# Final parameter products in wide views, log dt gradient as rows, w2 loads without touches: a joint forward and backward kernel on one core

## The chip, the cores and the metric

The kernel runs on one core of a Trainium2 chip. The metric is the device time of one execution in microseconds. TensorE multiplies matrices, VectorE and ScalarE work element by element, GpSimd (POOL in the profile) does some small element work and issues DMAs from a queue of its own, SyncE (SP) only issues DMAs, and ScalarE (ACT) can issue them as well.

## The reference

One call computes a forward pass and all gradients. The sizes are L = 2048 positions, D = 576 channels, N = 128 states and F = 4608 hidden units, and all tensors are bf16.

```python
xn = layernorm(x)                                     # over D
K[d, l] = Re sum_n C[d,n] * exp(dt[d]*A[d,n]*l) * dt[d]*B[d,n]   # dt = exp(log_dt), complex
s = causal_convolution(xn, K) + xn * Dskip            # along L, by FFT
h = silu(xn @ w1) * (xn @ w3)
out_0 = x + s * silu(h @ w2)
out_1 .. out_12 = gradients of out_0 against grad_out by
    x, A_re, A_im, B_re, B_im, C_re, C_im, log_dt, Dskip, w1, w3, w2
```

The gradients of A, B, C and log_dt end in small products. Four sums over the positions, S1 and S2 with real and imaginary parts, are made for each channel and state; out_2 to out_7 (576 x 128 each) are complex products of them with A, B, C and dt, and out_8 (576 values) is a sum over the states.

## The kernel before

All work is written once, stage by stage, for a list scheduler. `self.at(us)` gives the instructions that follow a planned time, and the scheduler puts each engine's instructions into an order by these times and by the dependences; on the chip each engine runs its list in that order. DMAs wait in the list of the engine that issues them (SP, POOL or ACT), and each of these has one queue.

The positions are 16 tiles of 128, D is five blocks of 128 channels (the last has 64), and F is 36 chunks of 128. The stages and the times they have in the profiled execution are these.

- *Prologue, 0 to 150 us.* Layer norm, the rates and the matrices of the Fourier transform.
- *Hidden layer and convolution kernel, 150 to 542.* `ffn_hidden` makes the two hidden products (matmul L719, gate tile `gu_t`, whose stores to `GI_dram` are issued by POOL, L728; hidden tile `h_t`, stored by SP). Beside it `ssm_kernel(0, 8.55)` generates the convolution kernel in 36 chunks that are planned 8.55 us apart; its last matmul (L500) ends at 516 us, and the hidden layer's last at 542.
- *Forward tail, 545 to 812.* `forward_tail` loads w2 in nine groups of four chunks (`w2g`, 590 KB each, issued by POOL, L771), loads the hidden tiles transposed (`hc`, SP), multiplies (`po`, L787), and makes the convolution in quarters (`spectra_quarter`, L609 and L582, with loads `cu`, L660, issued by POOL). A store of out_0 for each pair of tiles is issued by POOL, L849. The tile `goT` is cleared by POOL (L764) after the hidden layer, and the one-element copy L770 reads it.
- *Backward groups, 812 to 1647.* Gradients of w2, w1 and w3 (L1229, L1257, L1276), the backward convolution, and from 1331 us on the first 19 of 36 parameter chunks.
- *Input gradient, 1647 to 2017.* `phase6_inputs` makes 144 matmuls for each of the 16 tiles (L1336) into `px` or `pgw`, from transposed loads `guc` and `ggc` on SP. After a tile is done, VectorE adds it (L1346) and `ln_bwd_tile` makes the layer norm backward (L1376 to L1384) and stores out_1 from ACT (L1386). Between the matmuls stand the remaining 17 parameter chunks: 32 small matmuls each (L989) into `et_ps`, products on VectorE (L996, `pr_q`) and sums (L998) into `S_all`.
- *Final blocks.* `final_block` is a generator, one for each of the five blocks of channels, run at the chunk after which its sums are complete: block 0 after chunk 20, 3 after 30, 1 after 33, 2 and 4 after chunk 35, the last. It loads six `rates` (POOL, L1019), transposes the four sums (TensorE, L1023), copies them (ACT, L1025), makes the complex products one 128x128 plane at a time (VectorE, L1033 to L1038, scalings L1049, L1051, L1054), scales the outputs (VectorE, L1043 and L1045, into `gout`, two buffers) and stores them (POOL, L1016). The log dt gradient is collected as a column for each block in `glogdt`. After block 4 it is cast (L1074) and stored by two DMAs (POOL, L1077 and L1078) whose destination has consecutive 2-byte values on consecutive partitions.

The wait of the late w2 loads is written as a touch of the destination, which reads a tile that is cleared only after the hidden layer:

```python
if n >= 3:
    nc.vector.tensor_copy(out=t_[rem:rem + 1, 0, 0:1], in_=self.goT[0][rem:rem + 1, nfull, 0:1])
```

Of the kernel before, what the change touches and what calls it, by code (L numbers as in the profile page):

```python
# [60 lines left out]
class K:  # L61
# [669 lines left out]
    def forward_tail(self, T0, TB, TQ, gctx):  # L731
# [35 lines left out]
        for n, t_ in enumerate(w2g):  # L767
            self.at(T0 - 4 + 2.5 * n)
            if n >= 3:
                nc.vector.tensor_copy(out=t_[rem:rem + 1, 0, 0:1], in_=self.goT[0][rem:rem + 1, nfull, 0:1])  # L770
            nc.gpsimd.dma_start(out=t_[:], in_=aps["B_w2"][n * GRP * P:(n + 1) * GRP * P, :].rearrange(  # L771
                "(c p) d -> p c d", p=P))
# [53 lines left out]
        for i in range(LT):  # L826
# [15 lines left out]
            if i % 2 == 1:  # L842
# [3 lines left out]
                g_t = g_all[:, i0:i0 + 2, :]  # L846
                nc.vector.tensor_tensor(out=g_t, in0=g_t, in1=x_t[:], op=ALU.add)
                self.at(T0 + 54 + TB * i)
                nc.gpsimd.dma_start(out=out0[i0 * P:(i0 + 2) * P, :].rearrange("(t p) d -> p t d", p=P), in_=g_t)  # L849
# [17 lines left out]
    def ssm_bwd_params(self, chunk_at, final_at, out, big, S_all, ps):  # L867
        cfg = self.cfg
        D, LT = cfg.D, cfg.LT
        final = self.phase5_final(out, big, S_all, ps)  # L870
        with self.tc.tile_pool(name="g_k", bufs=1, side="right") as gkp, self.tc.tile_pool(name="g_t", bufs=3, side="right") as tqp, \
# [7 lines left out]
            for ch in range(D // 16):  # L879
                self.at(chunk_at(ch))  # L880
                self.param_chunk(ch, gz, S_all, tqp, qp, rp, ps)
                for c in final_at.get(ch, ()):
                    self.at(final_at[ch][c])
                    next(final[c])

# [115 lines left out]
    def phase5_final(self, out, big, S_all, ps2):  # L1001
        cfg = self.cfg
        fp = out.enter_context(self.tc.tile_pool(name="gf", bufs=1, side="right"))
        fo = out.enter_context(self.tc.tile_pool(name="gfo", bufs=2, side="right"))
        self.glogdt = big.tile([P, cfg.DT], FP32, name="glogdt")
        self.nc.vector.memset(self.glogdt[:], 0.0)
        self.rdt = big.tile([P, 1], FP32, name="rdt")
        return [self.final_block(c, do, dsz, fp, fo, big, S_all, ps2) for c, (do, dsz) in enumerate(cfg.dch)]

    def final_block(self, c, do, dsz, fp, fo, big, S_all, ps2):  # L1010
# [4 lines left out]
        tt, ts_ = nc.vector.tensor_tensor, nc.vector.tensor_scalar  # L1015
        store = lambda name, t_: nc.gpsimd.dma_start(out=aps[name][do:do + dsz, :], in_=t_[v])  # L1016
# [3 lines left out]
        Ar, Ai, Br, Bi, Cr, Ci = [rates[v, j] for j in range(6)]  # L1020
# [5 lines left out]
        S1r, S2r, S1i, S2i = [ST[v, k, :] for k in range(4)]  # L1026
        f = [fp.tile([P, N], FP32, name=f"f{n}")[v] for n in range(5)]
        acc = [fp.tile([P, 1], FP32, name=f"acc{n}")[v] for n in range(4)]
        dtc = self.dt_col[v, c:c + 1]
        Wr, Wi, t1, x, y = f  # L1030

        def pair(o, a, b, p, q, op):
            tt(out=o, in0=a, in1=b, op=ALU.mult)  # L1033
            tt(out=t1, in0=p, in1=q, op=ALU.mult)  # L1034
            tt(out=o, in0=o, in1=t1, op=op)  # L1035

        def dot(o, a, b):
            nc.vector.tensor_tensor_reduce(out=t1, in0=a, in1=b, scale=1.0, scalar=0.0, op0=ALU.mult, op1=ALU.add, accum_out=o)  # L1038

        def out_(o, name, neg):  # L1040
            ob = fo.tile([P, N], BF16, name="gout")
            if neg:
                ts_(out=ob[v], in0=o, scalar1=dtc, scalar2=-1.0, op0=ALU.mult, op1=ALU.mult)  # L1043
            else:
                ts_(out=ob[v], in0=o, scalar1=dtc, scalar2=None, op0=ALU.mult)  # L1045
            store(name, ob)

        pair(Wr, Cr, Br, Ci, Bi, ALU.subtract)
        ts_(out=Wr, in0=Wr, scalar1=dtc, scalar2=None, op0=ALU.mult)  # L1049
        pair(Wi, Cr, Bi, Ci, Br, ALU.add)  # L1050
        ts_(out=Wi, in0=Wi, scalar1=dtc, scalar2=None, op0=ALU.mult)  # L1051
        pair(x, Wr, S2r, Wi, S2i, ALU.subtract)
        pair(y, Wr, S2i, Wi, S2r, ALU.add)
        ts_(out=y, in0=y, scalar1=-1.0, scalar2=None, op0=ALU.mult)  # L1054
        out_(x, "out_2", False)
        out_(y, "out_3", False)
        dot(acc[0], x, Ar)
        dot(acc[1], y, Ai)
        tt(out=acc[0], in0=acc[0], in1=acc[1], op=ALU.add)
        dot(acc[2], S1r, Wr)  # L1060
        dot(acc[3], S1i, Wi)
        tt(out=acc[2], in0=acc[2], in1=acc[3], op=ALU.subtract)
        nc.vector.reciprocal(out=self.rdt[v], in_=dtc)
        tt(out=acc[2], in0=acc[2], in1=self.rdt[v], op=ALU.mult)
        tt(out=acc[0], in0=acc[0], in1=acc[2], op=ALU.add)
        tt(out=self.glogdt[v, c:c + 1], in0=acc[0], in1=dtc, op=ALU.mult)
        for (Xr, Xi, on_r, on_i) in ((Br, Bi, "out_6", "out_7"), (Cr, Ci, "out_4", "out_5")):
            pair(x, S1r, Xr, S1i, Xi, ALU.subtract)
            pair(y, S1r, Xi, S1i, Xr, ALU.add)
            out_(x, on_r, False)  # L1070
            out_(y, on_i, True)
# [409 lines left out]
```

## Time and profile before

| | us |
|---|---|
| time, median of three runs | 2052.34 |
| the three runs | 2048.55, 2052.34, 2052.43 |
| the profiled execution: time | 2052.34 |
| the profiled execution: span from the first to the last instruction | 2050.6 |
| outside the span | 1.7 |
| last matmul ends | 2016.8 |
| busy TensorE, VectorE, ScalarE, GpSimd | 1770.2, 1440.8, 996.1, 294.7 |

The mean clock that TensorE was granted is 0.951 of full speed. In the profile L with a number is a line of the kernel, an arrow between two tiles points from what is read to what is written, and an idle engine's wait is put down to the instruction or DMA that came last. "Landing" is the time from a DMA's issue to the arrival of its last byte. A row that begins with PE, DVE, ACT, POOL or SP belongs to TensorE, VectorE, ScalarE, GpSimd or SyncE, and PEld is the loading of weights into TensorE.

### The profile page before, as it was taken

To read this page: it belongs to the slowest core of one execution; us is meant where nothing else is said; L and a number is where in the kernel's file an instruction comes from. 1 tells how busy PE (TensorE), PEld (TensorE's weight loads), DVE (VectorE), ACT (ScalarE), POOL (GpSimd) and SP (SyncE) were. 2 spreads that over 40 slices of the span, in tenths; PEclk is the share of its full clock that TensorE was granted. 3 is DMA by queue.
4 is the path that set the end of the run, shared out by engine and by line. 5 is a ranking of instruction groups with operands and counts; after the bars stand their busy time and mean duration, and the time that the engine had idled before them with its cause. 6 is when DMAs were issued, how large, how long until landed. Compare 5 with 4: busy or idle time off the path is not lost. (4 is left out here: it accounts for less than half of the span.)

```text
span 2050.6 us, 41906 instructions
## 1 busy us (share of the span) xinstructions
PE 1770.2 (86%) x17103; PEld 1295.2 (63%) x17174; DVE 1440.8 (70%) x2777; ACT 996.1 (49%) x1672; POOL 294.7 (14%) x402
## 2 busy tenths in 40 slices
PE   2789999999779988889989899889988967989992
PEld 1444444444468866778778777767877845767672
DVE  7438888988267752486983868757978903698785
ACT  2768887888535553765666746434445200000000
POOL 4003333333222222000000000100000000010112
PEclk9899999999989999999999999989998988999997
DMA  3579888887986588655563655799998898999990
GB/s 84 180 278 327 288 287 307 305 289 274 213 211 166 149 193 190 175 170 171 167 177 118 178 161 157 201 251 202 242 183 215 214 198 177 215 184 234 216 176 14
DMA packets 608450, 417.11 MB, mean 203 GB/s; under 512 B 396993, under 2 KB 552705, under 8 KB 603521
## 3 DMA queue, kind: packets, MB, share of 16 engines
q1 hardware_dynamic: 545024, 278.11, 56.0%
q0 software_dynamic: 25952, 110.19, 16.7%
q10 hardware_dynamic: 37280, 26.14, 4.7%
q8 instruction: 134, 2.20, 0.5%
q14 instruction: 60, 0.48, 0.1%
HBM read 134.06 MB, written 188.01 MB: 157 GB/s over the span
## 5 line engine op out<-in xcount | busy, mean ns | idle before, releaser
L719 PE MATMUL pgu<-wmB_w,xnT 128*128 128x512 bf16 x1088 | 277.5, 384 | 10.1 <-issue 3.9
L1276 PEld LDWEIGHTS <-xn_bf 128*128 128x128 bf16 x2304 | 223.8, 98 | 30.6 <-issue 3.8
L1276 PE MATMUL pgw<-Y,xn_bf 128*128 128x256 bf16 x2048 | 232.1, 272 | 2.6 <-ACT gw L1278 1.8
L996 DVE TENSOR_TENSOR pr_q<-et_ps,pz 128x512 f32<-128x512 f32 x288 | 187.4, 684 | 43.8 <-PE et_ps L989 35.7
L1229 PE MATMUL ph<-w2T,goT 128*128 128x256 bf16 x1440 | 195.1, 285 | 18.3 <-ACT gh L1232 18.0
L719 PEld LDWEIGHTS <-xnT 128*128 128x128 bf16 x1152 | 103.7, 98 | 131.0 <-issue 30.1
L998 DVE TENSOR_REDUCE S_all<-pr_q 128x16 f32<-128x1024 f32 x144 | 175.3, 1217 | 1.5
L1235 DVE TENSOR_TENSOR Y<-gh,Y 128x1024 bf16<-128x1024 bf16 x128 | 86.6, 685 | 110.8 <-ACT gh L1232 108.7
L1229 PEld LDWEIGHTS <-goT 128*128 128x128 bf16 x1440 | 142.9, 102 | 30.9 <-issue 8.7
L1376 ACT ACTIVATE X<-X 128x576 f32<-128x576 f32 x16 | 10.9, 683 | 311.2 <-DVE X L1346 271.1
L787 PE MATMUL po<-w2g,hc 128*128 128x288 bf16 x1152 | 154.5, 292 | 7.2 <-DMA hc<-H_dram 7.2
L1278 ACT CAST gw<-pgw 128x256 bf16<-128x256 f32 x144 | 54.0, 377 | 198.9 <-PE pgw L1276 198.9
L1336 PEld LDWEIGHTS <-ggc 128*128 128x128 bf16 x1152 | 113.9, 100 | 50.8 <-DMA wTB<-in_B_w_dram 11.8
L1336 PEld LDWEIGHTS <-guc 128*128 128x128 bf16 x1152 | 114.1, 100 | 45.7 <-DMA guc<-GU_dram 14.6
L787 PEld LDWEIGHTS <-hc 128*128 128x128 bf16 x1152 | 113.3, 100 | 37.3 <-DMA hc<-H_dram 7.5
L1257 PE MATMUL pgw<-go_o,X 128*128 128x288 bf16 x896 | 121.5, 289 | 0.0
L1232 ACT CAST gh<-ph 128x512 bf16<-128x512 f32 x144 | 84.2, 617 | 58.0 <-PE ph L1229 38.5
L722 ACT ACTIVATE s_t<-pgu 128x512 bf16<-128x512 f32 x144 | 87.0, 606 | 51.6 <-PE pgu L721 50.9
L1257 PEld LDWEIGHTS <-X 128*128 128x128 bf16 x960 | 94.1, 99 | 24.4 <-issue 0.6
L467 DVE TENSOR_SCALAR m_k<-et_ps 128x512 int32<-128x512 int32 x108 | 74.0, 685 | 44.9 <-PE et_ps L466 44.7
L728 POOL DMA_DIRECT2D GI_dram<-gu_t x72 | 68.6, 953 | 227.1 <-DVE gu_t L724 189.7
L582 PEld LDWEIGHTS <-dSi 128*128 128x128 bf16 x768 | 77.3, 101 | 34.8 <-issue 34.0
(332 smaller groups left out, 4014.1 us busy)
## 6 DMA issues: line engine op xcount, KB each, us to landing
GI_dram<-gu_t POOLq DMA_DIRECT2D x72, 512.0 KB, 5.8
Y<-GI_dram POOLq DMA_DIRECT2D x19, 1024.0 KB, 6.2
H_dram<-h_t SPq DMA_DIRECT2D x72, 256.0 KB, 5.2
Q_dram<-q_k SPq DMA_DIRECT2D x36, 512.0 KB, 4.8
X<-GI_dram POOLq DMA_DIRECT2D x18, 1024.0 KB, 8.3
GU_dram<-Y SPq DMA_DIRECT2D x34, 512.0 KB, 4.3
GG_dram<-Y SPq DMA_DIRECT2D x30, 512.0 KB, 5.5
E_dram<-E_k SPq DMA_DIRECT2D x18, 768.0 KB, 3.7
```

The lines of the kernel that those rows point to most:

```text
L582: nc.tensor.matmul(pv, lhsT=mat[:, kt, sl], rhs=V[:, :, ri, kt, :], start=(i == 0), stop=(i == n - 1))
L719: nc.tensor.matmul(pgu[:, j], lhsT=xnT[:, c, ts], rhs=wm[w][:, c, :], start=(c == 0), stop=False)
L722: nc.scalar.activation(out=s_t[:, :, q, :], in_=pgu[:, 0].rearrange("p (g f) -> p g f", g=ng), func=ACT.Silu)
L787: nc.tensor.matmul(pos[k][:, pi_, 0:pw], lhsT=hcs[k][:, fi, :], rhs=w2[fi][:, po:po + pw], start=(fi == 0), stop=(fi == FT - 1))
L996: nc.vector.tensor_tensor(out=pr[:, r], in0=T[r][:], in1=pz[:, s + r, h * 8:h * 8 + 8, :][:, :, None, :] .to_broadcast([P, 8, 2, AV]), op= ...
L998: nc.vector.tensor_reduce(out=S_all[:, 2 * s:2 * s + 2, d0:d0 + 8].rearrange("p k d -> p d k"), in_=pr[:].rearrange("p r d k a -> p d k r ...
L1229: nc.tensor.matmul(ph[j][:, k, :].rearrange("p (a f) -> p a f", f=P), lhsT=lw, rhs=rh, start=(n == 0), stop=(n == nfull))
L1232: nc.scalar.copy(out=gh[:, j], in_=ph[j])
L1235: nc.vector.tensor_tensor(out=t_[:, sl], in0=gh.rearrange("p j t f -> p (j t) f"), in1=t_[:, sl], op=ALU.mult)
L1257: nc.tensor.matmul(pgw[pi_][:, 0:pw], lhsT=hn[:, tt, fl * P:(fl + 1) * P], rhs=go_o[:, tt, po:po + pw], start=(tt == 0), stop=(tt == LT - 1))
L1276: nc.tensor.matmul(pw_[:, 0:FG], lhsT=self.xn_bf[:, tt, c * P:(c + 1) * P], rhs=nat[:, tt, :], start=(tt == 0), stop=(tt == LT - 1))
L1336: nc.tensor.matmul(px[pi_][:, 0:pw], lhsT=act[:, fi, :], rhs=wT[ai][fi][:, po:po + pw], start=(fi == 0 and ai == 0), stop=(fi == FT - 1 an ...
```

## The change

Five things are changed.

1. The touch ahead of the w2 loads of groups 3 to 8 is removed; each load then waits only for the memory it writes to, which kernel generation used before.
2. For out_0 the sum is written to the tile that was loaded (`x_t`) instead of `g_all`, and the store is issued by SP instead of POOL, without a planned time of its own.
3. The planned times change: 8.7 instead of 8.55 us for each kernel-generation chunk, and for parameter chunks from 19 on a start of 1.4 instead of 1.5 tiles and a distance of 13.5 instead of 14.2 us.
4. `final_block` loads its rates one block ahead, makes the products of two planes with one instruction (a broadcast plane times two planes side by side, 128x256), leaves dt out of the products and applies it (dt, -dt or dt squared, prepared once in `dts`) when ScalarE writes the outputs into one of six `gout` buffers. The stores are issued by ACT. The log dt column of each block is transposed by TensorE into a row, copied by ScalarE and stored by ACT as one contiguous row for each block.
5. In `ln_bwd_tile` ScalarE adds the mean term to the residual gradient (two activations), and VectorE makes two scalar_tensor_tensor instructions in place of a tensor_scalar, a tensor_tensor and one scalar_tensor_tensor.

```diff
--- before.py
+++ after.py
@@ -766,8 +766,6 @@
         w2 = [w2g[fi // GRP][:, fi % GRP, :] for fi in range(FT)]
         for n, t_ in enumerate(w2g):
             self.at(T0 - 4 + 2.5 * n)
-            if n >= 3:
-                nc.vector.tensor_copy(out=t_[rem:rem + 1, 0, 0:1], in_=self.goT[0][rem:rem + 1, nfull, 0:1])
             nc.gpsimd.dma_start(out=t_[:], in_=aps["B_w2"][n * GRP * P:(n + 1) * GRP * P, :].rearrange(
                 "(c p) d -> p c d", p=P))
         for i0 in range(0, LT, 2):
@@ -843,10 +841,8 @@
                 i0 = i - 1
                 x_t = self.elp.tile([P, 2, D], BF16, name="gh6")
                 nc.gpsimd.dma_start(out=x_t[:], in_=xin[i0 * P:(i0 + 2) * P, :].rearrange("(t p) d -> p t d", p=P))
-                g_t = g_all[:, i0:i0 + 2, :]
-                nc.vector.tensor_tensor(out=g_t, in0=g_t, in1=x_t[:], op=ALU.add)
-                self.at(T0 + 54 + TB * i)
-                nc.gpsimd.dma_start(out=out0[i0 * P:(i0 + 2) * P, :].rearrange("(t p) d -> p t d", p=P), in_=g_t)
+                nc.vector.tensor_tensor(out=x_t[:], in0=g_all[:, i0:i0 + 2, :], in1=x_t[:], op=ALU.add)
+                nc.sync.dma_start(out=out0[i0 * P:(i0 + 2) * P, :].rearrange("(t p) d -> p t d", p=P), in_=x_t[:])
         fw.close()
 
     def ssm_bwd_conv(self, T0, TQ, ps):
@@ -868,6 +864,7 @@
         cfg = self.cfg
         D, LT = cfg.D, cfg.LT
         final = self.phase5_final(out, big, S_all, ps)
+        next(final[0])
         with self.tc.tile_pool(name="g_k", bufs=1, side="right") as gkp, self.tc.tile_pool(name="g_t", bufs=3, side="right") as tqp, \
                 self.tc.tile_pool(name="g_q", bufs=2, side="right") as qp, \
                 self.tc.tile_pool(name="g_r", bufs=1, side="right") as rp:
@@ -882,6 +879,9 @@
                 for c in final_at.get(ch, ()):
                     self.at(final_at[ch][c])
                     next(final[c])
+                    after = [n for m in sorted(final_at) for n in final_at[m]]
+                    if after.index(c) + 1 < len(after):
+                        next(final[after[after.index(c) + 1]])
 
     def conv_bwd_quarter(self, g, kp, zp, ps, T0, TQ):
         nc, cfg = self.nc, self.cfg
@@ -999,84 +999,81 @@
                                             in_=pr[:].rearrange("p r d k a -> p d k r a"), op=ALU.add, axis=AX.XY)
 
     def phase5_final(self, out, big, S_all, ps2):
-        cfg = self.cfg
+        nc, cfg = self.nc, self.cfg
         fp = out.enter_context(self.tc.tile_pool(name="gf", bufs=1, side="right"))
-        fo = out.enter_context(self.tc.tile_pool(name="gfo", bufs=2, side="right"))
-        self.glogdt = big.tile([P, cfg.DT], FP32, name="glogdt")
-        self.nc.vector.memset(self.glogdt[:], 0.0)
-        self.rdt = big.tile([P, 1], FP32, name="rdt")
-        return [self.final_block(c, do, dsz, fp, fo, big, S_all, ps2) for c, (do, dsz) in enumerate(cfg.dch)]
-
-    def final_block(self, c, do, dsz, fp, fo, big, S_all, ps2):
+        fo = out.enter_context(self.tc.tile_pool(name="gfo", bufs=1, side="right"))
+        self.dts = big.tile([P, 2, cfg.DT], FP32, name="dts")
+        nc.vector.tensor_scalar(out=self.dts[:, 0], in0=self.dt_col[:], scalar1=-1.0, scalar2=None, op0=ALU.mult)
+        nc.vector.tensor_tensor(out=self.dts[:, 1], in0=self.dt_col[:], in1=self.dt_col[:], op=ALU.mult)
+        return [self.final_block(c, do, dsz, fp, fo, S_all, ps2) for c, (do, dsz) in enumerate(cfg.dch)]
+
+    def final_block(self, c, do, dsz, fp, fo, S_all, ps2):
         nc, cfg = self.nc, self.cfg
         D, DT, N = cfg.D, cfg.DT, cfg.N
         aps = self.aps
         v = slice(0, dsz)
-        tt, ts_ = nc.vector.tensor_tensor, nc.vector.tensor_scalar
-        store = lambda name, t_: nc.gpsimd.dma_start(out=aps[name][do:do + dsz, :], in_=t_[v])
+        tt = nc.vector.tensor_tensor
         rates = fp.tile([P, 6, N], BF16, name="rates")
...
+        yield
+        Cr, Ci = rates[v, 4], rates[v, 5]
+        bc = rates[v, 2:6].rearrange("p (s r) n -> p s r n", r=2)
         pt = ps2.tile([P, 4, N], FP32, name="et_ps")
         for kd in range(4):
             nc.tensor.transpose(pt[0:dsz, kd, :], S_all[:, kd, do:do + dsz], self.ident_f[:])
         ST = fp.tile([P, 4, N], FP32, name="ST")
         nc.scalar.copy(out=ST[v], in_=pt[v])
...
+        S1r, S1i = ST[v, 0], ST[v, 2]
+        S2 = ST[v].rearrange("p (r s) n -> p s r n", s=2)[:, 1]
+        A, B = [fp.tile([P, 4, N], FP32, name=f"f{n}")[v] for n in range(2)]
+        acc = fp.tile([P, 4], FP32, name="acc")[v]
+        col = lambda a: a[:, None, :].to_broadcast([dsz, 2, N])
+
+        def cmul(o, t, ar, ai, b, neg=False):
+            tt(out=o, in0=col(ar), in1=b, op=ALU.mult)
+            tt(out=t, in0=col(ai), in1=b[:, ::-1], op=ALU.mult)
+            tt(out=o[:, 0], in0=o[:, 0], in1=t[:, 0], op=ALU.subtract)
             if neg:
-                ts_(out=ob[v], in0=o, scalar1=dtc, scalar2=-1.0, op0=ALU.mult, op1=ALU.mult)
+                nc.vector.scalar_tensor_tensor(out=o[:, 1], in0=o[:, 1], scalar=-1.0, in1=t[:, 1], op0=ALU.mult,
+                                               op1=ALU.subtract)
             else:
-                ts_(out=ob[v], in0=o, scalar1=dtc, scalar2=None, op0=ALU.mult)
-            store(name, ob)
-
-        pair(Wr, Cr, Br, Ci, Bi, ALU.subtract)
...
-        if c == DT - 1:
-            gl_bf = big.tile([P, DT], BF16, name="gl_bf")
-            nc.vector.tensor_copy(out=gl_bf[:], in_=self.glogdt[:])
...
+                tt(out=o[:, 1], in0=o[:, 1], in1=t[:, 1], op=ALU.add)
+
+        def dot(k, t, a, b):
+            nc.vector.tensor_tensor_reduce(out=t, in0=a, in1=b, scale=1.0, scalar=0.0, op0=ALU.mult, op1=ALU.add,
+                                           accum_out=acc[:, k:k + 1])
+
+        def store(k, names, src, scales):
+            for j, (name, s, sc) in enumerate(zip(names, src, scales)):
+                ob = fo.tile([P, N], BF16, name=f"gout{k + j}")
+                nc.scalar.activation(out=ob[v], in_=s, func=ACT.Copy, scale=sc)
+                nc.scalar.dma_start(out=aps[name][do:do + dsz, :], in_=ob[v])
+
+        dtc, ndt, dt2 = self.dt_col[v, c:c + 1], self.dts[v, 0, c:c + 1], self.dts[v, 1, c:c + 1]
+        U, X = A[:, 0:2], A[:, 2:4]
+        cmul(U, B[:, 0:2], Cr, Ci, bc[:, 0])
+        cmul(X, B[:, 2:4], U[:, 0], U[:, 1], S2, True)
+        store(0, ("out_2", "out_3"), (X[:, 0], X[:, 1]), (dt2, dt2))
+        dot(0, B[:, 0], X[:, 0], rates[v, 0])
+        dot(1, B[:, 1], X[:, 1], rates[v, 1])
+        dot(2, B[:, 2], S1r, U[:, 0])
+        dot(3, B[:, 3], S1i, U[:, 1])
+        tt(out=acc[:, 0:1], in0=acc[:, 0:1], in1=acc[:, 1:2], op=ALU.add)
+        tt(out=acc[:, 2:3], in0=acc[:, 2:3], in1=acc[:, 3:4], op=ALU.subtract)
+        nc.vector.scalar_tensor_tensor(out=acc[:, 0:1], in0=acc[:, 0:1], scalar=dtc, in1=acc[:, 2:3], op0=ALU.mult,
+                                       op1=ALU.add)
+        tt(out=acc[:, 0:1], in0=acc[:, 0:1], in1=dtc, op=ALU.mult)
+        gl = ps2.tile([P, 512], FP32, name="et_ps")
+        nc.tensor.transpose(gl[0:1, 0:dsz], acc[:, 0:1], self.ident_f[v, v])
+        row = fo.tile([1, P], BF16, name="glrow")
+        nc.scalar.copy(out=row[:, v], in_=gl[0:1, 0:dsz])
+        nc.scalar.dma_start(out=aps["out_8"][do:do + dsz].rearrange("(o p) -> o p", o=1), in_=row[:, v])
+        A4, B4 = [t_.rearrange("p (s r) n -> p s r n", r=2) for t_ in (A, B)]
+        for s in range(2):
+            cmul(A4[:, s], B4[:, s], S1r, S1i, bc[:, s])
+        store(2, ("out_6", "out_7", "out_4", "out_5"), [A4[:, s, r] for s in range(2) for r in range(2)],
+              (dtc, ndt) * 2)
         yield
 
     def backward(self, T0, TG, TQ, TX, gctx, mats):
@@ -1110,7 +1107,7 @@
                 self.wT_into(t[:], ai, 0, wT, lambda c: T2 - 160 + 12 * (2 * c + ai))
             T1 = T0 + 4 * TQ
             N1 = 19
-            chunk_at = lambda ch: T1 + 13.5 * ch if ch < N1 else T2 + TX * 1.5 + 14.2 * (ch - N1)
+            chunk_at = lambda ch: T1 + 13.5 * ch if ch < N1 else T2 + TX * 1.4 + 13.5 * (ch - N1)
             final_at = {20: {0: T2 + 4.5 * TX}, 30: {3: chunk_at(30) + 10}, 33: {1: chunk_at(33) + 10},
                         35: {2: chunk_at(35) + 9, 4: chunk_at(35) + 10}}
             self.ssm_bwd_params(chunk_at, final_at, out, fix, S_all, ps)
@@ -1377,12 +1374,13 @@
         mgx = sm.tile([P, 1], FP32, name="mgx")
         nc.vector.tensor_tensor_reduce(out=o1, in0=g, in1=xh, scale=1.0, scalar=0.0, op0=ALU.mult,
                                        op1=ALU.add, accum_out=mgx[:])
+        mgr = sm.tile([P, 1], FP32, name="mgr")
+        nc.scalar.activation(out=mgr[:], in_=mg[:], func=ACT.Copy, scale=self.rstd[:, i:i + 1])
+        nc.scalar.activation(out=t, in_=go_t, func=ACT.Identity, bias=mgr[:, 0:1], scale=1.0)
         nmgx = sm.tile([P, 1], FP32, name="nmgx")
         nc.vector.tensor_scalar(out=nmgx[:], in0=mgx[:], scalar1=-invD, scalar2=None, op0=ALU.mult)
-        nc.vector.tensor_scalar(out=t, in0=xh, scalar1=nmgx[:, 0:1], scalar2=mg[:, 0:1], op0=ALU.mult, op1=ALU.add)
-        nc.vector.tensor_tensor(out=t, in0=g, in1=t, op=ALU.add)
-        nc.vector.scalar_tensor_tensor(out=o1, in0=t, scalar=self.rstd[:, i:i + 1], in1=go_t,
-                                       op0=ALU.mult, op1=ALU.add)
+        nc.vector.scalar_tensor_tensor(out=g, in0=xh, scalar=nmgx[:, 0:1], in1=g, op0=ALU.mult, op1=ALU.add)
+        nc.vector.scalar_tensor_tensor(out=o1, in0=g, scalar=self.rstd[:, i:i + 1], in1=t, op0=ALU.mult, op1=ALU.add)
         nc.scalar.dma_start(out=out1[i * P:(i + 1) * P, :], in_=o1)
 
 
@@ -1442,7 +1440,7 @@
             with tc.tile_pool(name="f_w", bufs=2) as wp, \
                     tc.tile_pool(name="f_gu", bufs=3, side="right") as gup, \
                     tc.tile_pool(name="f_ps", bufs=3, space=bass.MemoryType.PSUM) as fps:
-                k.ssm_kernel(0, 8.55)
+                k.ssm_kernel(0, 8.7)
                 k.ffn_hidden(wp, gup, fps, 0, 9.5)
         gctx = ExitStack()
         k.forward_tail(315, 11.5, 34, gctx)
```

More of the change, by code (lines that the diff above doesn't have):

```diff
@@ L1019, in final_block @@
             nc.gpsimd.dma_start(out=rates[v, j], in_=aps[name][do:do + dsz, :])
-        Ar, Ai, Br, Bi, Cr, Ci = [rates[v, j] for j in range(6)]
+        yield
+        Cr, Ci = rates[v, 4], rates[v, 5]
+        bc = rates[v, 2:6].rearrange("p (s r) n -> p s r n", r=2)
         pt = ps2.tile([P, 4, N], FP32, name="et_ps")
@@ L1025, in final_block @@
         nc.scalar.copy(out=ST[v], in_=pt[v])
[L1026 to L1041, printed above, removed]
+        S1r, S1i = ST[v, 0], ST[v, 2]
[3 more added lines that the diff above has]
+        col = lambda a: a[:, None, :].to_broadcast([dsz, 2, N])
@@ L1049, in final_block @@
[L1049 to L1071, printed above, removed]
@@ L1072, in final_block @@
-        if c == DT - 1:
-            gl_bf = big.tile([P, DT], BF16, name="gl_bf")
-            nc.vector.tensor_copy(out=gl_bf[:], in_=self.glogdt[:])
-            nfull = D // P
-            with nc.allow_non_contiguous_dma(reason="small vector store"):
-                nc.gpsimd.dma_start(out=aps["out_8"][0:nfull * P].rearrange("(c p) -> p c", p=P), in_=gl_bf[:, 0:nfull])
-                nc.gpsimd.dma_start(out=aps["out_8"][nfull * P:D].rearrange("(p o) -> p o", o=1),
-                                    in_=gl_bf[0:D - nfull * P, nfull:nfull + 1])
+                nc.vector.scalar_tensor_tensor(out=o[:, 1], in0=o[:, 1], scalar=-1.0, in1=t[:, 1], op0=ALU.mult,
+                                               op1=ALU.subtract)
+            else:
+                tt(out=o[:, 1], in0=o[:, 1], in1=t[:, 1], op=ALU.add)
```

## Prediction

> **What bounds the kernel now.** I read the page from the shares down, then the chain at the end, the DMA issues of the last 70 us, and four stretches by their windows. First the engines, and two rows of the 40 slices:
>
> ```profile
> PE 1770.2 (86%) x17103; PEld 1295.2 (63%) x17174; DVE 1440.8 (70%) x2777; ACT 996.1 (49%) x1672; POOL 294.7 (14%) x402
> ...
> PE   2789999999779988889989899889988967989992
> DMA  3579888887986588655563655799998898999990
> ```
>
> TensorE sets the pace nearly everywhere. Its weak places are the start, 500–600 us, 750–800 us and the last slice; only the last one is empty. The chain of waits shows what stands there:
>
> ```profile
> 2017.09 0.83 DVE X L1346 x2
> ...
> 2020.41 0.79 DVE X L1384
> 2021.25 0.49 DVE f L1033 x2
> ...
> 2029.66 0.45 POOL out_dram L1077
> 2030.11 0.33 issue
> 2030.44 0.53 POOL out_dram L1078
> ...
> 2032.00 0.52 POOLq L1476
> ```
>
> After the last matmul (2016.8) VectorE makes the last layer norm backward, then all products of parameter block 4, and only then POOL stores the log dt gradient. How long the stores take is in the DMA issues from 1980 us on (tile, queue, count, KB each, median us to landing):
>
> ```profile
> out_dram<-gout POOLq DMA_DIRECT2D x10, 32.0 KB, 1.7
> out_dram<-X ACTq DMA_DIRECT2D x2, 144.0 KB, 1.8
> out_dram<-gout POOLq DMA_DIRECT2D x6, 16.0 KB, 2.4
> ...
> out_dram<-gl_bf POOLq DMA_DIRECT2D x1, 1.0 KB, 17.2
> out_dram<-gl_bf POOLq DMA_DIRECT2D x1, 0.1 KB, 16.6
> ```
>
> The two smallest stores are the slowest: element by element, they land at 2030.44 + 0.53 + 16.6 = 2047.6, and the span ends 3.0 later. The windows (us, PE busy, PEld, DVE, ACT, POOL, clock, DMA share, GB/s):
>
> ```profile
> 1760.00:2017.00 257.00, 237.67 (x2218) 184.95 (x2215) 213.97 (x454) 11.45 (x29) 22.56 (x42) 0.97 0.98 191
> 2017.00:2031.50 14.50, 0.00 (x0) 0.00 (x0) 12.81 (x56) 0.78 (x2) 6.70 (x14) 0.66 0.09 27
> 2031.50:2050.60 19.10, 0.00 (x0) 0.00 (x0) 0.00 (x0) 0.00 (x0) 1.02 (x2) 0.50 0.01 2
> 530.00:600.00 70.00, 48.48 (x431) 37.04 (x430) 33.77 (x68) 26.20 (x50) 18.51 (x33) 0.85 0.91 231
> ```
>
> So 33.8 us have no matmul at all, and 19.1 of these no engine at work. Before the end TensorE idles 19.3 of 257; around the end of the FFN 21.5 of 70. The waits of TensorE (engine, tile, line, releaser: us in total, times, longest) in 500–600, 735–815 and 1760–2020 us name the largest:
>
> ```profile
> PE et_ps L582 <- DVE V L609: 14.6, 2, 12.6
> ...
> PE po L787 <- DMA hc<-H_dram: 7.2, 2, 6.2
> ...
> PE et_ps L989 <- DVE pr_q L996: 8.8, 10, 3.1
> ```
>
> **The end.** In the new order block 4's products stand on VectorE ahead of the last tile's layer norm, which is now its last five instructions; block 4's stores are ahead of the last tile's on ACT. What follows the last matmul: L1346 twice as now, to 2017.92; the dot product and its read, 0.76 + 0.12, 2018.80; nmgx, 0.15, 2018.95; the first scalar_tensor_tensor by L1384's row, 0.8, 2019.75. Beside it ACT does the mean (0.68 + 0.19, from 2017.94), the small scaling (0.2, the size of the accumulator read) and the Identity pass (0.68, L1376's row), to about 2020.0 with hand-overs; ACT now decides there. Second scalar_tensor_tensor to 2020.85, issue 0.34 by ACT, landing 1.8: 2023.0; the same 3.0 to the span's end: 2026.0. **Gain 24.6 us.**
>
> Does block 4 fit ahead of it? Its last chunk is now followed by 260 matmuls; a tile of 144 takes 17.6 us, so 0.122 each, 31.9 us. The chunk's second half takes VectorE 4 x 0.6 + 2 x 1.13 plus block 2's pieces; then block 2 about 5 us, block 4 with layer norm 14 about 8. Block 2's scalar is ready about 21.6 us before the end, and its transpose on TensorE stands 22.3 before: a wait of 0 to 1. Block 4's is ready at 12.9, the transpose at 12.5: none. Its row store goes out some 11 us before the last matmul ends; even at the old 17.2 us it would land 6 us after it, together with the last tile's store. A contiguous run of 256 B is what each row of a gout store has (128 values of 2 B), and 64 of these landed in 2.4, so I take 2.4 from the gout row, not 17.2.
>
> The page "DMA: Bandwidth & Descriptors" of the Trainium skill, under "Anatomy of one DMA", fits a GpSimd DMA by 2.0 us plus bytes over 436 GB/s. By that the old vector stores would have cost 2.0, the end before would have been near 2037, and this change would gain about 11 us there instead of 24.6. The trace has 17.2 and 16.6, and decides.
>
> **Parameter blocks and layer norm.** A block on VectorE was 24 products or sums and 9 scalings at 0.20 from start to start, 4 dots at 0.29, six tiny ones at 0.1: 8.4 us, and waits for the two gout buffers (7.6 and 2.4 in this stage). Now it is four pairs of 128x256 products, two sums or differences for each, 4 dots: 4 x (2 x 0.34 + 2 x 0.20) + 1.2 + 0.5 = 5.9; 0.34 is an estimate from 0.28 for 128x128 and 0.45 for 128x288. The six output scalings go to ACT, busy 11 of 257 us there, with six buffers and stores on its queue. Behind a scaling that waits for its product or for a store of the block before (landed after 1.7) stand the next block's copy and layer norm passes; blocks come 10 us or more apart, so nothing. The layer norm loses 0.58 + 0.76 and gains 0.81: about 0.4 after overlap, 16 times. In all VectorE saves some 4 x 2.5 + 6 = 16 us, and the gout waits. Most of that is no gain, as TensorE waits for it only 8.8 us. The five transposes of log dt cost 0.1 each and a wait of 0 to 3. Rates are loaded a block earlier on POOL, idle there. **Denser chunks** (13.5 for 14.2, start 1.8 us earlier) put more VectorE work and more DMA, already at 0.98, into the same matmuls. I take **-4** for the end of TensorE: half of the 8.8. Bounds: -12 (all of 8.8 and the issue waits), +8 (five waits of 1.5).
>
> **The w2 loads.** The six touches go (0.1 us each). Six loads of 590 KB stop waiting for the end of the FFN (546.5) and start as kernel generation frees their memory, 7.25 FFN tiles of 2.15 us, 15.7 us, ahead of it. On POOL they now stand ahead of the last four gate stores (L728) and, seven of them, ahead of the first cu loads (L660). Now the second cu load, issued 549.6 behind three w2 loads, lands about 569, and this is the 12.6 us above. Gain: up to 12. Loss: the sixth gate store waits behind five loads, 2.95 MB; at the 140 GB/s that this queue had in 500–600 us (14.01 MB) that is 21 us, and gu_t has three buffers, so the ninth pair could hold TensorE 0 to 12 us. Both are near; I take **0 to -2**, bounds -10 and +12. Generation planned 5.4 us longer moves work between two stages where TensorE is 97% busy: nothing.
>
> **out_0.** The stores leave POOL, where they wait for VectorE (9.4 and 8.3 us) in front of other loads, for SP, where they wait in front of the transposed loads of hidden tiles 13 to 15 (TensorE lost 7.2 us to such a load). Sum 0, bounds -6 and +6. "Issuing engines are not separate DMA queues" of the same page says that all queues end on the same 16 engines, so by it the move gains no bandwidth and the term is 0; no row here separates the two.
>
> Sum against the profiled execution (2052.3, span 2050.6 and 1.7 around it; it is also the median): 2052.3 - 24.6 - 4 - 2 = **2022**.
>
> **Rivals.**
> *The load block hurts (slower).* One mechanism: nine w2 loads in a row in POOL's queue hold the last gate stores and the cu loads. To cancel 28.6 us, and 4 more to be seen, cu must land some 33 us later than 569. Seven loads, 4.13 MB, from about 526: that takes under 55 GB/s, where the queue had 140. Time about 2058. Against it: those loads now start some 20 us earlier. 0.08.
> *TensorE's end moves out.* The denser chunks starve the gate loads or the log dt transposes wait: +8 there, +0 to +10 in the transition and the middle; end gain kept, 2052.3 - 24.6 + 8 + 0 to 10: 2036 to 2046. For it: DMA share 0.98. 0.24.
> *The transition and the middle give all they can*: -10 and -6 more than nothing, with -8 at the end: 2002 to 2012. For it: 12.6 us in one wait. 0.13.
> *The loads don't start earlier*, since their memory is not free: 2024, within the forecast's own range.
> The forecast, 2012 to 2035, has 0.55.
>
> **Numbers.** Time 2022. The range 2006 to 2041 leaves out the slower rival and the ends of the two others. Less than 0.2% (4 us) can't be told from no change by a measurement of this kernel: the slower rival gives slower 0.08; the far end of the second, beyond 2045, gives same 0.05; the rest is faster, 0.87.
>
> **What would show it.** Right: the last DMA is out_1's last store, landing some 6 us after the last matmul; no gl_bf rows; log dt rows landing in about 2 us; TensorE's waits for pr_q below 8.8 us; the 12.6 us wait smaller. Wrong: after the last matmul more than 12 us, or TensorE's last matmul beyond 2025, or a new wait of L719 for gu_t above 10 us.

## The result and the profile after

The changed kernel took 2021.8 us (median of four, 2013.96 to 2025.81) against 2050.45 for the kernel before (2048.11 to 2052.43): a ratio of 0.9856, interval 0.9823 to 0.9889. The forecast, 2022 in 2006 to 2041, holds the time, but it holds it by two errors that cancel. Times here and below are medians over all executions, and each ratio leaves out the slow ones of either kernel, so it can differ from the ratio of two medians. The profiled execution took 2021.15, its span is 2019.1. The page's rows for the engines and two of the slices:

```profile
PE 1766.5 (87%) x17108; PEld 1295.5 (64%) x17179; DVE 1421.0 (70%) x2660; ACT 1024.7 (51%) x1739; POOL 270.2 (13%) x362
...
PE   2789999999899988989899998889979967988887
DMA  3589888797966597365563655798998998999992
```

The holes at 500–600 us and in the last slice are smaller. TensorE's three slices ahead of the last, 9 each before, now read 8: a new loss. The starts of the first and last matmuls of some lines cut both spans into the same five stretches (us):

| stretch | before | after | change |
|---|---|---|---|
| start to the last hidden-layer matmul (L719) | 541.1 | 530.3 | -10.8 |
| to the last w2 matmul (L787, now L785) | 270.7 | 256.5 | -14.2 |
| to the first wT matmul into pgw (L1336, now L1333) | 870.7 | 869.1 | -1.6 |
| to the last input-gradient matmul | 334.0 | 356.6 | **+22.6** |
| to the end of the span (the tail) | 34.1 | 6.6 | -27.5 |
| span | 2050.6 | 2019.1 | -31.5 |

The windows (us, busy PE, PEld, DVE, ACT, POOL, clock, DMA share, GB/s), the first two of the same lengths as those shown before:

```profile
530.00:600.00 70.00, 58.93 (x662) 51.23 (x661) 49.54 (x97) 36.28 (x79) 21.19 (x42) 0.93 0.79 241
1756.00:2013.00 257.00, 219.25 (x2033) 167.85 (x2028) 199.77 (x366) 31.16 (x76) 12.67 (x24) 0.95 0.93 174
2013.00:2019.10 6.10, 0.00 (x0) 0.00 (x0) 3.09 (x7) 1.85 (x4) 0.00 (x0) 0.71 0.07 24
```

TensorE idles 37.8 of the 257 us ahead of the end, where it idled 19.3. The whole fourth stretch, before and after:

```profile
1682.50:2016.50 334.00, 300.11 (x2729) 233.24 (x2726) 240.35 (x497) 14.36 (x35) 22.06 (x41) 0.96 0.97 189
```

```profile
1655.90:2012.50 356.60, 305.09 (x2733) 234.82 (x2731) 232.95 (x439) 42.27 (x100) 12.67 (x24) 0.94 0.94 178
```

So of the 22.6 us lost there 17.6 are idle time of TensorE. The other 5.0 are busy time, at a granted clock of 0.94 instead of 0.96; in the kernel with the first product late, below, it is 298.5 us at 0.97. No run here separates the clock from the idle time. TensorE's waits in 500–600 and in 1760–2020 us, and below them the waits of VectorE and of ScalarE from 1740 us on, name the cause:

```profile
PE et_ps L626 <- ACT gu_t L724: 8.5, 1, 8.5
PE et_ps L582 <- DVE V L609: 2.3, 3, 0.8
...
PE et_ps L989 <- DVE pr_q L996: 26.1, 18, 8.1
```

```profile
DVE f L1034 <- ACT gout L1050: 30.9, 4, 11.1
...
DVE pr_q L996 <- DMA pz<-PZ_dram: 7.0, 2, 6.5
```

```profile
ACT gout L1050 <- DMA guc<-GU_dram: 25.1, 3, 11.4
...
ACT gout L1050 <- DMA ggc<-GG_dram: 8.6, 1, 8.6
```

The 12.6 us for V are gone, 8.5 for a gate tile have come. The waits for pr_q went from 8.8 to 26.1, and those for guc from 4.5 to 8.0. Before, VectorE's longest waits of this kind in 1750–2017 us were for its two output buffers:

```profile
DVE gout L1045 <- DMA out_dram<-gout: 7.3, 6, 2.3
...
DVE f L1033 <- DMA rates<-in_A_C_re_dram: 2.4, 2, 1.8
DVE gout L1043 <- DMA out_dram<-gout: 2.4, 3, 1.4
```

Now VectorE waits for ScalarE, and ScalarE for a transposed load that SP issued. The chain of waits between 1949 and 1972 us shows one whole case:

```profile
1949.42 15.36 DMA guc<-GU_dram
1964.85 0.35 ACTq L1051
1965.29 0.39 ACTq L1051
1965.73 0.41 ACT gout L1050
1966.16 0.43 DVE f L1034
1966.59 1.13 DVE S_all L998
...
1970.77 1.21 DVE pr_q L996 x2
```

A gradient store on ACT's queue (L1051) is not issued until SP's load of guc has landed. The scaling of the last output stands behind it on ScalarE and still reads the product tile f. VectorE's first product of the *next* block (L1034) writes that tile, and it stands in VectorE's list ahead of the sums of a parameter chunk. Behind the sums stand the chunk's next products (`pr_q`, L996), and TensorE waits for these to get its et_ps buffer back. That a store waits for a load of another engine is set by the compiled program: 25 of the 30 gradient stores wait there, besides for their data, for the DMA that used their completion counter before them, and the DMAs of SP and ACT share eight such counters. In the trace 24 of these waits are instructions of their own (`L1051 ACTq EVENT_SEMAPHORE x24`).

The end is as forecast: block 4 is done, and the last tile's layer norm is what is left (timeline of VectorE and of ACT).

```profile
2012.71 0.82 DVE L1343 TENSOR_TENSOR X<-pgw,X 128x288 f32<-128x288 f32 x2 [9.69 <-PE pgw L1333]
...
2015.54 0.82 DVE L1383 SCALAR_TENSOR_TENSOR X<-X,rstd 128x576 bf16<-128x576 f32 x1
```

```profile
2014.70 0.78 ACT L1379 ACTIVATE X<-X,mgr 128x576 f32<-128x576 bf16 x1
2016.39 0.34 ACTq L1384 DMA_DIRECT2D out_dram<-X  x1
```

### The profile page after: what moved, and what is told of

Its sections match the earlier page's. It is cut to its first block, busy times and chain, and to the rows that moved or that the text cites. A ratio compares the mean times of both kernels' runs of the same rounds, so it can differ in the third digit from the quotient of the medians.

```text
span 2019.1 us, 41885 instructions
## 1 busy us (share of the span) xinstructions
PE 1766.5 (87%) x17108; PEld 1295.5 (64%) x17179; DVE 1421.0 (70%) x2660; ACT 1024.7 (51%) x1739; POOL 270.2 (13%) x362
## 5 line engine op out<-in xcount | busy, mean ns | idle before, releaser
L719 PE MATMUL pgu<-wmB_w,xnT 128*128 128x512 bf16 x1088 | 273.4, 380 | 6.4 <-issue 3.2
L996 DVE TENSOR_TENSOR pr_q<-et_ps,pz 128x512 f32<-128x512 f32 x288 | 186.4, 684 | 48.8 <-PE et_ps L989 37.7
L1226 PE MATMUL ph<-w2T,goT 128*128 128x256 bf16 x1440 | 195.3, 285 | 18.3 <-ACT gh L1229 18.1
L719 PEld LDWEIGHTS <-xnT 128*128 128x128 bf16 x1152 | 103.2, 98 | 124.1 <-issue 18.9
L785 PE MATMUL po<-w2g,hc 128*128 128x288 bf16 x1152 | 156.1, 294 | 7.8 <-DMA hc<-H_dram 7.8
L1333 PEld LDWEIGHTS <-ggc 128*128 128x128 bf16 x1152 | 114.2, 100 | 52.0 <-DMA wTB<-in_B_w_dram 11.8
L1333 PEld LDWEIGHTS <-guc 128*128 128x128 bf16 x1152 | 114.5, 101 | 49.2 <-DMA guc<-GU_dram 17.2
L785 PEld LDWEIGHTS <-hc 128*128 128x128 bf16 x1152 | 113.8, 100 | 39.0 <-DMA hc<-H_dram 8.2
L989 PE MATMUL et_ps<-gz,qT 128*128 128x64 bf16 x1152 | 57.6, 198 | 50.0 <-DVE pr_q L996 41.5
L989 PEld LDWEIGHTS <-qT 128*128 128x128 bf16 x1152 | 48.8, 101 | 79.0 <-DVE pr_q L996 38.3
```

What stands on the lines that cost most here:

```text
L719: nc.tensor.matmul(pgu[:, j], lhsT=xnT[:, c, ts], rhs=wm[w][:, c, :], start=(c == 0), stop=False)
L785: nc.tensor.matmul(pos[k][:, pi_, 0:pw], lhsT=hcs[k][:, fi, :], rhs=w2[fi][:, po:po + pw], start=(fi == 0), stop=(fi == FT - 1))
L989: nc.tensor.matmul(T[r][:, dd].rearrange("p k (f t) -> p (k f) t", f=2), lhsT=qT[:, dl, :], rhs=gK[:, r, :, :, dl, :].rearrange("p k f t - ...
L996: nc.vector.tensor_tensor(out=pr[:, r], in0=T[r][:], in1=pz[:, s + r, h * 8:h * 8 + 8, :][:, :, None, :] .to_broadcast([P, 8, 2, AV]), op= ...
L1226: nc.tensor.matmul(ph[j][:, k, :].rearrange("p (a f) -> p a f", f=P), lhsT=lw, rhs=rh, start=(n == 0), stop=(n == nfull))
L1333: nc.tensor.matmul(px[pi_][:, 0:pw], lhsT=act[:, fi, :], rhs=wT[ai][fi][:, po:po + pw], start=(fi == 0 and ai == 0), stop=(fi == FT - 1 an ...
```

## The experiments

Theory A after this reading: the stores on ACT, together with a first product that stands early, cost stage 4 its 22 us. Rival B: the denser plan of the chunks does. Rival C: the transfers of stage 4 take their time whenever it starts. On the three chips of these runs the kernel before took 2037 to 2077 us, so a few us are read from the stretches of the profiles, not from medians. "Stage 4" and "the stretch" are the fourth of the table, up to the last input-gradient matmul.

**Stores back on POOL.**

```diff
-                nc.scalar.dma_start(out=aps[name][do:do + dsz, :], in_=ob[v])
+                nc.gpsimd.dma_start(out=aps[name][do:do + dsz, :], in_=ob[v])
```

> The changed kernel with one edit: the six gradient stores of each final block are issued by POOL again; the scalings stay on ScalarE and the log dt row stays on ACT. Theory A (stores on ACT's queue wait for transposed loads of SP, ScalarE's next scaling waits behind them, VectorE waits for it with its first product of the next block, TensorE for VectorE): VectorE's waits for gout fall from 30.9 us to under 5, TensorE's waits for pr_q from 26.1 to about 9, the last matmul comes 15 us earlier: 2006. Rival B (the denser parameter chunks cost the time): 2022, the waits for pr_q stay. Rival C (stage 4 is held by its DMA traffic, whenever it starts): 2020 to 2024, with the waits changing their names only.

Measured: 2017.0, ratio to the kernel before 0.9789 (0.9724 to 0.9854); the stretch before the end 347.9 instead of 356.6. The waits for gout are gone from VectorE's list, but the stores now stand among the loads of the rates on POOL, and the same product waits for those:

```profile
DVE f L1034 <- DMA rates<-in_A_C_re_dram: 18.1, 3, 6.3
```

TensorE's waits for pr_q are 18.2 us, not about 9, and the stretch is 8.7 us shorter where A forecast 15: the queue is not the whole cause. That the place of the product is the other part is tested below.

**The old plan of the chunks.** `T2 + TX * 1.5 + 14.2 * (ch - N1)` again, all else as changed.

> The changed kernel with the planned times of the parameter chunks from 19 on as before (start 1.5 tiles, distance 14.2). Theory A: the stall behind the stores on ACT stays, 2022 plus 0 to 8, since the last blocks lie nearer to the end. Rival B (denser chunks cost 17 us): 2007. Rival C: 2022.

Measured: 2013.3, ratio 0.9762 (0.9662 to 0.9862); the stretch is 336.9 and the tail 12.7, since block 4's products now run among those of the last layer norm; both together are 349.6 instead of 363.2, near what B has. B is not shown by this: VectorE's waits for gout fell as well (30.9 to 7.5). Only a run with the denser plan and without those waits can tell.

**The first product late.** With S2*B first, then times C, the first product reads the sums, so the scheduler can't put it ahead of them.

```diff
-        cmul(U, B[:, 0:2], Cr, Ci, bc[:, 0])
-        cmul(X, B[:, 2:4], U[:, 0], U[:, 1], S2, True)
+        cmul(U, B[:, 0:2], ST[v, 1], ST[v, 3], bc[:, 0])
+        cmul(X, B[:, 2:4], Cr, Ci, U, True)
```

> The changed kernel with the products in another order, so that the first product of a block reads S2 (S2*B, then times C; the log dt sum over S1*B times C): scalings and stores stay on ACT, the denser plan stays. The first product then stands behind the chunk's sums on VectorE. Theory A: waits of f for gout and rates fall from 35 us to under 8, TensorE's waits for pr_q to about 10, and stage 4 from the first pgw matmul to the last takes 333 to 340 instead of 356.6: about 2003. Rival B (the denser plan by itself costs): 350 to 357, 2018 to 2022.

Measured: 2000.5 (1992 to 2004), ratio 0.9736 (0.968 to 0.9791); the stretch is 330.6. The waits of TensorE, VectorE and ScalarE:

```profile
PE et_ps L989 <- DVE pr_q L996: 9.2, 14, 5.0
```

```profile
DVE f L1033 <- DMA rates<-in_A_B_im_dram: 0.7, 1, 0.7
```

```profile
ACT gout L1049 <- DMA guc<-GU_dram: 18.1, 2, 9.8
```

ScalarE still waits 18.1 us for guc, but this no longer lengthens the stretch: nothing that TensorE needs stands behind it now. The denser plan is unchanged, and the stretch is shorter than before (334.0): the plan by itself does not cost the time. B falls, and C with it, as the stage starts where it did (its first pgw matmul at 1659.5 us, 1655.9 in the changed kernel).

**Scalings on VectorE, stores on POOL.**

```diff
-                nc.scalar.activation(out=ob[v], in_=s, func=ACT.Copy, scale=sc)
-                nc.scalar.dma_start(out=aps[name][do:do + dsz, :], in_=ob[v])
+                nc.vector.tensor_scalar(out=ob[v], in0=s, scalar1=sc, scalar2=None, op0=ALU.mult)
+                nc.gpsimd.dma_start(out=aps[name][do:do + dsz, :], in_=ob[v])
```

> The changed kernel with the output scalings of the final blocks on VectorE and their stores on POOL again (wide products, six buffers and rows kept). Theory A (VectorE's first product of the next block waits for what reads the last block's products): the 30.9 us of waits of f for gout go, those for rates stay (4 to 18), stage 4 from the first pgw matmul to the last takes 340 to 350 instead of 356.6. Rival B (the denser plan): 350 to 360.

Measured: 1999.2, ratio 0.9755 (0.9687 to 0.9823), the stretch 335.2: with 30 more instructions on VectorE the stage is 21 us shorter, and shorter than A had it. Over most kernels this stretch follows VectorE's waits for f, gout and pz there (us); the last four rows are runs of the next parts:

| kernel | VectorE's waits | stretch |
|---|---|---|
| first product late | 9.9 | 330.6 |
| before | 14.7 | 334.0 |
| scalings on VectorE | 16.0 | 335.2 |
| old plan | 18.0 | 336.9 |
| stores on POOL | 28.1 | 347.9 |
| changed | 41.9 | 356.6 |
| changed, again | 39.9 | 356.7 |
| changed, out_0 on POOL | 39.8 | 357.9 |
| changed, log dt as a column | 25.1 | 336.9 |
| before, log dt as rows | 20.9 | 345.0 |

The last two lie off the line by some 8 us, so the sum of the waits is not all that counts. In five profiles with the changed kernel's code in this stage the stretch is 351.5 to 357.9; in the two with the product late it is 330.6 and 332.6. Old plan, late product, scalings on VectorE and the column each take away most of the loss alone: it needs the store's wait, the early product and the times at which the blocks run together.

**The changed kernel again**, beside these.

> The changed kernel itself once more, on the chip of the next three runs: 2014 to 2026. Its profile shows how far the stretches of one kernel vary: the end of the hidden layer and start of the forward tail by up to 18 us (8.5 and 26.5 us of waiting for a gate store were seen in two kernels with the same code there), the last stretch by a few us.

Measured: 2018.6 (2004.6 to 2026.5), ratio 0.9823 (0.9752 to 0.9893); the stretch is 356.7, the tail 6.6. The late first product is 18 us faster in the same session.

**The w2 loads.** First the touches left out of the kernel before, then put back into the changed one, then the changed one with `k.ssm_kernel(0, 8.55)`.

> The kernel before with the touches of the w2 loads left out, nothing else. If these loads are the cause of the earlier forward tail: the 12.6 us wait for V goes, the last w2 matmul comes 15 to 20 us earlier, and since the end of the old kernel is unchanged the time is 2050 - 18 = 2032. If the tail's gain needs the out_0 stores off POOL as well: 2040 to 2046. If stage 4 absorbs what comes early (rival C): 2046 to 2050 with a longer stage 4.

> The changed kernel with the touches of the w2 loads put back. If they are worth the 25 us of the forward tail: 2022 + 18 to 25 = 2040 to 2047. If stage 4 absorbs it (rival C, the end is set by loads that do not start earlier): 2022 to 2028.

> The changed kernel with kernel generation planned at 8.55 us a chunk again. If the longer plan only moves work between two busy stages, as the prediction has it: the same within the variation of the forward tail, V of the last convolution quarter ends at 712 to 732. If it is what lets the w2 loads start without a stall (fewer hidden tiles, and so fewer gate stores, are left behind them): the hidden layer ends near 542 with TensorE waiting 10 to 20 us for gate tiles, V ends near 743, and the time is 10 to 30 us longer than the changed kernel's.

Measured, in this order: 2043.7 (ratio 0.9935, 0.9905 to 0.9965), 2040.7 (0.9887, 0.9847 to 0.9927) and 2038.9 (0.9921, 0.9872 to 0.9969). The times at which V's last matmul ran, us:

| | touches | no touches |
|---|---|---|
| 8.55 us a chunk | 736.3 (before) | 743.2, 737.7 |
| 8.7 us a chunk | 742.0 | 712.1 (changed); 712.0 to 717.1 in six others, 731.3 in one |

Neither edit makes V earlier alone; together they gain 24. The upper left and the first number beside it are of the kernel before, the rest of the changed one; each number is one profile. The hidden layer's end goes by the plan alone: 531 with the touches back, 535 with the short plan back. The times say the same more weakly: with one of the two undone the changed kernel's ratio is 0.9887 and 0.9921, against 0.9856 and 0.9823, and the intervals overlap. The first forecast missed: the wait for V stayed (14.3 us in one). That this kernel is still 0.65% faster comes from elsewhere in its profile: its third stretch took 857.9 us instead of 870.7. Over the 14 profiles this stretch ran from 854 to 878 us; what sets it stays open. TensorE's waits in 525–610 us of the first and the third kernel show why:

```profile
PE et_ps L582 <- DVE V L609: 15.7, 3, 14.3
PE et_ps L626 <- DVE gu_t L724: 11.6, 1, 11.6
PE pgu L719 <- ACT gu_t L724: 7.9, 1, 7.9
```

```profile
PE et_ps L626 <- DVE gu_t L724: 13.5, 1, 13.5
PE et_ps L582 <- DVE V L609: 9.6, 3, 8.3
```

Without the touches the short plan ends generation at 510 us with 31 and 25 us of the hidden layer left; the long one at 515 with 15. So six gate stores, not four, come after the first w2 load in POOL's order, and the loads for the convolution go out later: the first cu load is issued at 556.9 and 552.4 us, in the changed kernel here:

```profile
532.15 0.55 POOL L660 DMA_DIRECT2D cu<-UH_dram  x1
```

The waits of ScalarE and VectorE from 520 and 525 to 570 us in the first kernel, and of ScalarE in the changed one:

```profile
ACT gu_t L724 <- DMA GI_dram<-gu_t: 16.0, 3, 10.5
DVE h_t L725 <- DMA H_dram<-h_t: 19.1, 2, 16.5
```

```profile
ACT gu_t L724 <- DMA GI_dram<-gu_t: 7.5, 1, 7.5
```

The second row is of stores of the hidden tile, which SP issues. So POOL's order is not all: stores of both engines land late beside the w2 loads, and how much each part costs is not shown. V at 731.3 is the kernel with gradient stores on POOL; there, with the same code, POOL stood still for a landing:

```profile
548.07 0.91 POOL L728 DMA_DIRECT2D GI_dram<-gu_t  x1 [22.53 <-DMA w2g<-in_B_w_dram]
```

This wait was 2.2 in the changed kernel's profile, where TensorE waited 8.5 us for a gate tile and here 26.5: the rival of the prediction is real, at a varying size.

**The w2 loads in another order.** On top of the late first product, loads 3 to 8 are planned 8 us later, so POOL issues the last gate stores earlier among them.

> The kernel with the first product late (2000), and the w2 loads from the fourth on planned 8 us later, so that POOL issues the sixth gate store after three w2 loads instead of five and the seventh after four instead of seven. If the 8.5 to 11 us in which TensorE waits for a gate tile at the end of the hidden layer come from those loads: this wait falls under 5, V ends 4 to 8 us earlier, 1994 to 1997. If the same bytes must land before the convolution anyway: the wait moves to V (L609) and the time stays at 2000.

Measured: 2016.6 (1988.6 to 2035.8), ratio 0.9737 (0.9673 to 0.9801). The wait for the gate tile fell to 5.0, a new one came, and V ended at 724.8:

```profile
PE po L785 <- DMA hc<-H_dram: 10.6, 1, 10.6
PE et_ps L626 <- ACT gu_t L724: 5.0, 1, 5.0
```

The ratio is that of the late first product alone (0.9736): no gain. The wait moved, though not to V (L609) as the second forecast had it, but to a load of hidden tiles (hc).

**out_0 back on POOL.** Sum and store as before, all else as changed.

> The changed kernel with the out_0 sum and store as before (in place, issued by POOL at its planned time). In seven kernels so far the stretch from the last V matmul to the last w2 matmul was 75 us with the stores on POOL and 64 to 75 with them on SP, so: 70 to 76 here, and a time 0 to 8 us longer than the changed kernel's. If the move is worth nothing: 68 to 72 and the same time.

Measured: 2020.9 (2004.7 to 2045.9), ratio 0.9805 (0.9756 to 0.9854); V to the last w2 matmul 71.8 us, against 74.7 and 70.4 in two profiles of the changed kernel. No effect that these runs can tell. Over all 14 profiles this distance is 72 to 86 with the stores on POOL (four) and 64 to 75 with them on SP (ten), so a gain of a few us isn't excluded.

**The log dt stores.** First the changed kernel with the column and its two element-wise stores after block 4, then the kernel before with the rows alone.

```diff
-        gl = ps2.tile([P, 512], FP32, name="et_ps")
-        nc.tensor.transpose(gl[0:1, 0:dsz], acc[:, 0:1], self.ident_f[v, v])
...
+                nc.gpsimd.dma_start(out=aps["out_8"][0:nfull * P].rearrange("(c p) -> p c", p=P), in_=gl_bf[:, 0:nfull])
```

> The changed kernel with the log dt gradient stored as before: a column for each block, and after block 4 two element-wise stores of POOL. Block 4's products stay ahead of the last layer norm. The prediction: the stores go out about 11 us before the last matmul ends and land 17 us later, together with out_1's last store, so the tail after the last matmul stays at 6 to 10 us and the time within 4 us of the changed kernel's (2019 to 2022). Rival (the form of the store makes the end): tail 20 us or more, 2034.

Measured: 1997.4 (1980.4 to 2011.9), ratio 0.968 (0.9634 to 0.9725). The DMA issues after 1940 us, and POOL's timeline:

```profile
out_dram<-gl_bf POOLq DMA_DIRECT2D x1, 1.0 KB, 18.0
out_dram<-gl_bf POOLq DMA_DIRECT2D x1, 0.1 KB, 17.4
```

```profile
1965.56 0.79 POOL L1079 DMA_DIRECT2D out_dram<-gl_bf  x1 [7.64 <-DVE f L1038]
1966.34 0.54 POOL L1080 DMA_DIRECT2D out_dram<-gl_bf  x1
```

The stores still take 18 us, but start 10 ahead of the last matmul (1975.7): the tail is 9.9. And against the expectation the kernel is faster than the changed one (0.9823 and 0.9856, intervals that do not meet its own): without the five transposes, row copies and row stores VectorE waits 13.1 us for gout instead of 30.9, and the stretch is 336.9. In this profile the rows cost more on ACT (some 20 us) than they gain at the end (3.3).

> The kernel before with one edit: the log dt gradient of each block is transposed by TensorE and stored as a row by ACT; block 4's products stay behind the last layer norm. The last store is then a gradient store of POOL at 2032.0 + 0.5, landing in 2.4: tail 2032.5 + 2.4 + 3.0 - 2016.8 = 21 us instead of 34, time 13 us shorter than the kernel before. Rival (the order alone makes the end): tail 30 us or more.

Measured: 2054.5 (2036.7 to 2077.4), ratio 0.9991 (0.9954 to 1.0028). The tail is 20.4 instead of 34.1, as expected; the time didn't show it. In its profile the stretch to the last matmul took 345.0 instead of 334.0 (VectorE's waits for its two gout buffers 16.4 instead of 9.7), and the two stretches ahead of it were 9.0 and 4.6 us longer. Whether the rows cause that in the old kernel stays open.

## Why the prediction was right, and where it was wrong

*The end, right.* Forecast -24.6, measured -27.5. Block 4 fitted ahead of the last layer norm; its last chunk ran 34 us ahead of the last matmul (31.9 forecast), and TensorE waited 2.2 us in all for log dt. The size was off by the tail: from the issue of out_1's last store to the span's end 2.7 us passed, not 0.34 + 1.8 + 3.0. Landing counts from the issue's start, so the 0.34 was in the 1.8 already, and the 3.0, read from the old kernel's end, did not carry over. That the *order* counts most is shown by the column store (tail 34.1 to 9.9); the rows alone, in the old order, give 20.4, and beside the order they are worth 3.3. The full order needs the denser plan: with the old one block 4 runs among the last layer norm, and the tail is 12.7. The landing of the rows, 2.4 in the forecast, is in no profile.

The Trainium skill (DMA: Bandwidth & Descriptors, "Anatomy of one DMA") gives a GpSimd DMA a fixed part of 2.0 us. The element-wise stores here don't agree: they took 18.0 and 17.4 us.

*Products, right.* A 128x256 product starts 0.33 us after the one before it (1989.09 and 1989.42 in VectorE's timeline), as estimated (0.34). The forecast's sum for a block is 6.0, not 5.9. VectorE's busy time fell by 19.8 where 16 was forecast.

*Stores on ACT, wrong.* The step "blocks come 10 us or more apart, so nothing" failed. It looked at ScalarE's busy time (11 of 257) and at the stores' own landing (1.7), not at what a store on that queue can wait for, nor at the next block's first product, which stood in VectorE's list ahead of the chunk. Measured +22.6 in the place of -4, outside the bound of +8. The runs show in its place a store that waits for SP's load, the scaling behind it, and the early product behind that: with that product late the stretch is 330.6 instead of 356.6. The second rival had the stage right (the end of TensorE moves out) but the wrong cause.

*The w2 loads and the plan, wrong in size.* The forecast was 0 to -2 with a bound of -10; the first two stretches gave -25. The step that took "Generation planned 5.4 us longer" for nothing failed: with the short plan back, V's last matmul moves from 712.1 to 737.7. The loads need that room. The mechanism forecast for the loss, gate stores behind w2 loads, was there (8.5 us in the changed kernel, 26.5 in the kernel with stores on POOL), and the first mechanism of gain as well (12.6 to 0.8). The second cu load of the old kernel landed at 566.1, not about 569; no term hangs on it.

*out_0, not contradicted*: forecast 0, and no effect clear of the profiles' variation.

The sum came out by luck, because +22.6 met -25. Read stretch by stretch, the forecast was wrong on three of five: the first two and the fourth.

## What to carry to other kernels

Before a store is moved to another engine's queue, list what it waits for there and what stands behind it on that engine, and follow it to the buffers' next writer: the cost was less in the store itself than in a product that a list scheduler had put early because its operands were ready. Make such an instruction depend on data that comes late, and the wait loses its victim. Edits that share a queue (loads and the plan that frees their memory) are tested together and apart; alone each of these two left V no earlier than before.

## What had not been expected of the hardware

Two element-wise stores of 1.0 and 0.1 KB took 17.2 and 16.6 us in the kernel before and 18.0 and 17.4 in another. In the kernel before the DMA engines were 1% busy meanwhile. ScalarE stood up to 11.4 us behind a store of its own queue that waited for a transposed load issued by SP. With the same code for the w2 loads and gate stores on POOL, the wait of a gate store's issue was 2.2 us in one profile and 22.5 in another. The granted clock of the fourth stretch was 0.94 with 51.5 us of TensorE idle and 0.97 with 32.1.
